# Separate use records in the linear branch, a gate with one transpose, and a new order, in a gated mix of softmax and linear attention

## The chip, the cores and the metric

The kernel runs on one core of one Trainium2 chip. The metric is device time in microseconds (us) from one execution; the median of several is compared. The core has five engines that run side by side and wait for one another by semaphores: TensorE (PE, matrix multiply), VectorE (DVE), ScalarE (ACT), GpSimd (POOL) and SyncE (SP, which issues most of the DMAs).

## The reference

One input x (2048 tokens, 512 features) goes through two attention branches with 32 heads of 16 features, and a gate mixes the results.

```python
# branch A: softmax attention
qkv = x @ wqkv                                   # 512 -> 3 * 512
p = softmax(q @ k.T * 16 ** -0.5)                # 32 heads, 2048 x 2048 each
a = (p @ v) @ wo
# branch B: linear attention; B_x is not used, x is the same
phi = lambda t: concat(softmax(t @ w_phi), softmax(-(t @ w_phi)))   # 32 features a head
kv, z = phi(k).T @ v, phi(k).sum(tokens)
b = (phi(q) @ kv / (phi(q) @ z + 1e-6)) @ wo
# gate
g = sigmoid((x * gate_w).sum(-1))
out = g * a + (1 - g) * b
```

Everything is bf16 at the inputs and the output. The bulk of it is the exponential of 32 x 2048 x 2048 scores.

## The kernel before, in words

**Softmax branch.** The scores are made transposed, keys on the partitions. A *unit* is one head's tile of 128 keys by 512 queries, one bank of PSUM. Four heads share the rows of TensorE, so four units make a *position* p; there are 512 positions (4 query chunks x 8 groups of four heads x 16 key tiles), and 2048 units. The loop runs over positions: scores (`_qk`, matmul line 988), exponential (`_exp`, line 1039), and the product with the values (`_pv`, line 1108), which adds up over the 16 key tiles of a group in one bank. Five banks are a ring for the scores; the ring is used in instructions of three and two units by turns (`GROUPS`), so ScalarE takes 1536 and 1024 columns by turns. The other three banks serve everything else.

**Units on VectorE.** A share of the units is not given to ScalarE. `SHARES` says how many of each group of 16 positions; `SOON` names four early ones. `_vector_batch` takes up to `NB` = 5 such units: line 887 scales the scores into the bits of a number (tile `vt`), `_cubic` (lines 911 to 915) makes a cubic of the fraction in `vf` and `vu`, and line 897 puts the two together. The values' product then reads `vu`. The last units of a group wait on TensorE for these tiles.

**Linear branch.** `_b_fuse` multiplies the key and query weights with `w_phi`, in place in `WB`. `_b_part` makes both softmaxes of a block of two or four token tiles on VectorE: the power of two apart from the remainder (lines 1300 and 1302, the remainder in `vf`, shared with the vector batches), a tree of maxima and one of minima (lines 1305 and 1309), their ends (line 1312, into `brec`), the differences (line 1315), a polynomial (lines 1320 to 1327), its two halves put out (lines 1329 and 1330), the sums, and their inverses. Keys come first (`_b_keys`, six calls), queries later (`_b_queries`, four calls).

**Gate.** `_gate` multiplies x with the gate's weights spread over 128 columns, a chunk of 512 tokens at a time: four matmuls into a bank, a transpose of 32 x 32 blocks on VectorE (line 805), and a copy of one column of each block (line 808). Two multiplications, an exponential on ScalarE (line 816) and an addition end it.

**The order of the work.** Nothing is written down in its final order. Each piece of work is an `Op` with an engine, a cost, a priority (`prio`, mostly the position at which it is due) and a release (`rel`, a position before which it isn't looked at). `Plan.order` then plays the execution through with these costs, engine by engine, and fixes the queue of each engine; the engines run their queues strictly in that order. `Buf` objects record who wrote and who read a tile; `Plan.op` turns the records into dependencies, also between two operations of one engine, which are waits on that engine's own semaphore. A DMA's landing is estimated in `_land`; for a plain load of `size` megabytes:

```python
self.loaded = max(o.end + 1.5, self.loaded) + o.size / 0.31
o.lat = self.loaded - o.end + (0.85 if self.loaded > 4.5 else 0.4)
```

The loads are in `_loads`. On SP, after the loads of x, come `WB` for the values (release 6) and the queries (8), the gate's weights (`gw`, release 6), the three larger pieces of the softmax weights (`WA`, columns from 128 on, release `XREL`), and the two output weights `WoA` and `WoB` (release 12). A query block of the softmax branch is projected in `_proj_q` (matmuls of line 681 into `qraw`, line 759, then eight small DMAs on SP, line 761).

The constants that the change sets: `LEAD`, `EARLY`, `SDUE` (when a vector batch is due), `QDUE`, `VPRIO`, `VREL`, `TPRIO` (when query projections, vector batches and normalisations are due), `XREL`, `KD`, `VD`, `KREL`, `VREL0` (loads and first projections), `FIRST` and `LAST` (sizes of the first and last vector batches), `OREL` (release of the last output tiles), `K0`, `SK`, `Q0`, `SQ` (positions of the linear branch's key and query parts).

Of the kernel before, what the change touches and what calls it, by code (L numbers as in the profile page):

```python
# [7 lines left out]
ALU = mybir.AluOpType  # L8
AX = mybir.AxisListType

P = 128
# [6 lines left out]
F32, BF16 = dt.float32, dt.bfloat16  # L18
# [349 lines left out]
class _Kernel:  # L368
# [46 lines left out]
    def _memory(self, ctx):  # L415
# [19 lines left out]
        self.gwb = sb("gwb", [P, 4, P], BF16)  # L435
        self.gh = sb("gh", [P, 2, NQC, 16], F32)
        self.gz = sb("gz", [P, NQC, 16], F32)
# [59 lines left out]
    def _loads(self):  # L497
# [17 lines left out]
        def load_wa(s, part, eng, prio, rel=-99):  # L515
            lo, hi = (0, P) if part == 0 else (P, D)
            self.dma(eng, f"wa{s}{part}", lambda e: e.dma_start(
                self.WA[:, s, :, lo:hi], WA3[:, :, D * s + lo:D * s + hi]), writes=[self.b_WA[s][part]], prio=prio,
                cost=0.54, rel=rel, size=0.131 if part == 0 else 0.393)

        def load_wb(s, prio, rel=-99):
# [20 lines left out]
                 writes=[self.b_gw], prio=-4, cost=0.53, rel=6, size=0.016)  # L542
# [245 lines left out]
    def _gate(self):  # L788
        op, NQC = self.plan.op, self.NQC
        b_gwb, last = Buf(), []  # L790
        op("POOL", lambda e: e.tensor_copy(self.gwb[:], self.gw[:, :, None].to_broadcast([P, 4, P])), 1.0,
           reads=[self.b_gw], writes=[b_gwb], name="gwb", prio=15)
        z = self.gz[:]
        for qc in range(NQC):
            job = Job()

            m = None
            for c in range(4):
                def mm(e, c=c, qc=qc, job=job):
                    return e.matmul(self._bank(job), self.gwb[:, c, :], self.xT[:, 4 * qc:4 * qc + 4, c],  # L800
                                    start=(c == 0), stop=(c == 3))
                m = op("PE", mm, self.c_pe(512), reads=[self.b_xT[qc], b_gwb], deps=[m], name="gate", prio=18 + qc,
                       rel=12, acquire=None if c else job)
            k = qc % 2
            t = op("DVE", lambda e, k=k, job=job: e.transpose(
                self.T1[:, k].rearrange("p b d -> p (b d)"), self._bank(job)), 0.65, deps=[m], name="gate_t",
                prio=18 + qc, writes=[self.b_T1[k]], release=job)
            last.append(op("DVE", lambda e, qc=qc, k=k: e.tensor_copy(self.gz[:, qc], self.T1[:, k, :, 0]), 0.2,
                           reads=[self.b_T1[k]], name="gate_c", prio=18 + qc))
        flat = self.gh[:].rearrange("p r q b -> p (r q b)")  # L810
        col = z.rearrange("p q b -> p (q b)")
        for r, sign in ((0, -1.0), (1, 1.0)):
            last.append(op("DVE", lambda e, r=r, sign=sign: e.tensor_scalar(
                self.gh[:, r].rearrange("p q b -> p (q b)"), col, sign, None, op0=ALU.mult), 0.2,
                deps=list(last), name="gate_z", prio=22))
# [12 lines left out]
    SHARES = (0, 2, 1, 8, 1, 8, 3, 4, 10, 3, 7, 6, 10, 4, 12, 3,  # L828
              2, 11, 10, 5, 13, 4, 7, 6, 14, 11, 4, 14, 6, 12, 14, 9)
# [5 lines left out]
    def _plan_vector(self):  # L835
# [9 lines left out]
        for k in range(n):  # L845
            at = (2 * k + 1) * 9 // (2 * n)
            self.away.append(4 * (self.NT * last + 4 * (at // 3) + at % 3 + 1) + 3)
# [328 lines left out]
    K0, SK, Q0, SQ = 17.0, 9.25, 178.0, 14.75  # L1176
    PAIRS = 8
    SOON = (8, 17, 18, 21)
    SDUE = 37

    def _branch_b(self):
# [5 lines left out]
        self.b_bsum, self.b_brec = B(), B()  # L1187
# [71 lines left out]
    def _b_part(self, s, t0, nt, slot, due):  # L1259

        op = self.plan.op
# [23 lines left out]
        rest = self.vf[:, 0:nt].rearrange("p n q -> p (n q)").rearrange("p (a v) -> p a v", v=64)  # L1285
# [12 lines left out]
        def dve(name, cost, fn, reads, writes, off=1):  # L1298
            op("DVE", fn, cost, reads=reads, writes=writes, name=name, prio=due + off)
        dve("b_grid", four(h), lambda e: e.tensor_scalar(up, signs(flat)[:, :, 0], OCTAVE, OCTAVE, op0=ALU.add,  # L1300
                                                         op1=ALU.subtract), b, [b_vt], 0)
        dve("b_rest", two(h), lambda e: e.tensor_tensor(rest, signs(flat)[:, :, 0], up, ALU.subtract), [*b, b_vt], [b_vf], 0)
        ends = ((0, ALU.max, -127.0 * 128), (1, ALU.min, 127.0 * 128))
        for s_, of, _ in ends:
            dve("b_max", two(h // 2), lambda e, s_=s_, of=of: e.tensor_tensor(tree[:, :, s_], up[:, :, 0:32], up[:, :, 32:64], of),
                [b_vt], b, 0)
        for m in (16, 8, 4):
            for s_, of, _ in ends:
                dve("b_max", two(8 * nt * m), lambda e, m=m, s_=s_, of=of: e.tensor_tensor(  # L1309
                    tree[:, :, s_, 0:m], tree[:, :, s_, 0:m], tree[:, :, s_, m:2 * m], of), b, b, 0)  # L1310
        for s_, _, bias in ends:
            dve("b_top", 0.066 + 0.0167 * nt, lambda e, s_=s_, bias=bias: e.tensor_scalar(
                top.rearrange("p (a s i) -> p a s i", s=2, i=4)[:, :, s_], tree[:, :, s_, 0:4], bias, None, op0=ALU.add),
                b, [b_brec], 0)
# [4 lines left out]
            ALU.subtract), [b_vt, b_brec], [b_vt])  # L1319
        dve("b_square", two(h), lambda e: e.tensor_tensor(even, rest, rest, ALU.mult), [b_vf], b)  # L1320
        dve("b_slope", four(h), lambda e: e.tensor_scalar(odd, even, ODD / r, 1 - ODD * c, op0=ALU.mult, op1=ALU.add),
            b, b)
        dve("b_even", four(h), lambda e: e.tensor_scalar(even, even, 128 * EVEN / r, 64 - 128 * EVEN * c,
                                                         op0=ALU.mult, op1=ALU.add), b, b)
        dve("b_odd", two(h), lambda e: e.tensor_tensor(odd, odd, rest, ALU.mult), [*b, b_vf], b)
        dve("b_part", two(h), lambda e: e.tensor_tensor(rest, even, odd, ALU.add), b, [b_vf])
        dve("b_part", two(h), lambda e: e.tensor_tensor(odd, even, odd, ALU.subtract), b, b)
        outs = signs(flat.bitcast(U16))
        dve("b_out", two(h), lambda e: e.tensor_tensor(outs[:, :, 0], down, rest, ALU.add), [b_vt, b_vf], b)
        dve("b_out", two(h), lambda e: e.tensor_tensor(outs[:, :, 1], odd, up, ALU.subtract), [b_vt, *b], b)  # L1330
# [251 lines left out]
```

## Time and profile before

| | |
|---|---|
| median of 3 runs | 840.32 us (840.21 to 841.15) |
| the profiled execution, whole | 842.38 us |
| its span, first to last instruction | 838.9 us |
| ScalarE busy | 826.7 us, 733 instructions |
| VectorE busy | 809.9 us, 1055 instructions |
| TensorE busy | 803.5 us, 8800 matmuls |
| granted TensorE clock | 1.00 |
| DMA | 20.01 MB, mean 24 GB/s |

The profile is one execution. Rows that group instructions read: line, engine, operation, output <- input, shapes, xcount | busy us, mean ns of one | idle us of the engine just before them, and what ended most of it. A record's length runs on into the next instruction's, so the distance of two starts, not the mean, is what one instruction costs in a row of them. Rows in order of time read: start, length, what, and in brackets the idle time before and what ended it. ACTq and SPq are the queues from which ACT and SP issue DMAs.

### The profile page before, as it was taken

How to read it: one execution, taken by the hardware profiler on the slowest of the kernel's cores; microseconds unless marked ns; L12 is line 12 of the kernel's file. 1: busy time of each engine (PE TensorE's matmuls, PEld its weight loads, DVE VectorE, ACT ScalarE, POOL GpSimd, SP SyncE). 2: the span in 40 equal slices, each digit the busy share in tenths (PEclk: the TensorE clock that was granted, in tenths of full speed). 3: DMA queues.
4: the chain of work that ended last, by engine and by line, in shares of the span. 5: the costliest groups of instructions: out<-in, count | busy, mean ns of one | idle time of the engine just before them, and what ended most of it. 6: DMA issues, size and time to landing. Idle time of an engine off the chain costs nothing.

```text
span 838.9 us, 19684 instructions
## 1 busy us (share of the span) xinstructions
PE 803.5 (96%) x8800; PEld 265.3 (32%) x8800; DVE 809.9 (97%) x1055; ACT 826.7 (99%) x733; POOL 8.1 (1%) x14
## 2 busy tenths in 40 slices
PE   9999999999999999999999999999999999999998
PEld 4334233233322322232223222332223332222344
DVE  5999999999999999999999989999999999999996
ACT  7999999999999999999999999999999999999997
POOL 3000000000000000000000000000000000000000
PEclk9999999999999999999999999999999999999999
DMA  9600000000000000030003000320002110000000
GB/s 227 183 1 3 5 2 7 1 2 8 2 7 2 8 1 8 2 65 19 1 15 81 14 8 2 57 52 1 8 2 52 33 32 2 2 7 2 2 2 27
DMA packets 49027, 20.01 MB, mean 24 GB/s; under 512 B 38704, under 2 KB 48944, under 8 KB 48944
## 3 DMA queue, kind: packets, MB, share of 16 engines
q1 hardware_dynamic: 48272, 18.58, 9.9%
q8 instruction: 68, 1.11, 0.6%
q10 hardware_dynamic: 672, 0.20, 0.1%
q14 instruction: 15, 0.12, 0.1%
HBM read 6.31 MB, written 2.10 MB: 10 GB/s over the span
## 4 chain that ended last, share of the span: by engine, by line
ACT 75%; DVE 16%; PE 4%; DMA 2%; SPq 2%; issue 0%
ACT ET L1039 75%; DVE vt L887 2%; DVE vu L897 2%; PE ps L988 2%; DVE vf L914 1%; DMA WA<-in_A_wqkv_dram 1%; PE ps L1117 1%; DVE vu L915 1%; DVE bq L1272 1%; DVE vf L911 1%; DMA WB<-in_B_wqkv_dram 1%; DVE vt L1315 1%; PE ps L1108 1%; SPq L604 1%; DVE bq L1309 1%; DVE V L783 1%
## 5 line engine op out<-in xcount | busy, mean ns | idle before, releaser
L1039 ACT ACTIVATE ET<-ps 128x1536 bf16<-128x1536 f32 x728 | 824.4, 1381 | 2.8 <-PE ps L988 2.3
L988 PE MATMUL ps<-qT,kT 32*128 32x512 bf16 (+2 forms) x2248 | 318.3, 364 | 26.8 <-ACT ET L1039 20.6
L1117 PE MATMUL ps<-kT,zero 128*32 128x512 bf16 (+1 forms) x3100 | 259.9, 383 | 0.0
L1108 PE MATMUL ps<-ET,V 128*32 128x512 bf16 (+2 forms) x1993 | 196.3, 364 | 0.7 <-DVE vt L887 0.4
L988 PEld LDWEIGHTS ps<-qT,kT 32*128 32x128 bf16 x2248 | 84.0, 91 | 305.0 <-ACT ET L1039 217.6
L887 DVE TENSOR_SCALAR vt<-ps 128x512 uint32<-128x512 f32 x224 | 145.1, 678 | 4.5 <-PE ps L988 4.0
L897 DVE SCALAR_TENSOR_TENSOR vu<-vt,vu 128x2560 int16<-128x2560 uint32 (+2 forms) x47 | 126.4, 2690 | 0.5
L1117 PEld LDWEIGHTS ps<-kT,zero 128*32 128x32 bf16 x3100 | 70.2, 94 | 109.0 <-issue 82.5
L1108 PE MATMUL ps<-vu,V 128*32 128x512 bf16 (+1 forms) x255 | 84.1, 360 | 0.0
L1108 PEld LDWEIGHTS ps<-ET,V 128*32 128x32 bf16 x1993 | 56.1, 95 | 58.4 <-issue 31.0
L915 DVE TENSOR_TENSOR vu<-vu,vf 128x2560 f16<-128x2560 f16 (+2 forms) x49 | 67.8, 1385 | 0.5
L914 DVE TENSOR_TENSOR vf<-vf 128x2560 f16<-128x2560 f16 (+2 forms) x49 | 67.8, 1385 | 0.2
L911 DVE TENSOR_SCALAR vf<-vt 128x2560 f16<-128x2560 uint8 (+2 forms) x47 | 66.7, 1418 | 0.0
L681 PE MATMUL ps<-WB,xT 128*128 128x512 bf16 x192 | 55.4, 383 | 1.1 <-DVE T L1161 1.0
L913 DVE TENSOR_SCALAR vu<-vf 128x2560 f16<-128x2560 f16 (+2 forms) x49 | 37.6, 767 | 0.2
L681 PE MATMUL ps<-xT,WA 128*128 128x512 bf16 (+1 forms) x124 | 35.3, 379 | 1.5 <-DMA WA<-in_A_wqkv_dram 1.3
L1108 PEld LDWEIGHTS ps<-vu,V 128*32 128x32 bf16 x255 | 22.4, 96 | 13.0 <-issue 8.4
L1161 DVE STREAM_TRANSPOSE T<-ps 128x512 f32<-128x512 f32 (+1 forms) x35 | 23.1, 660 | 2.1 <-PE ps L1108 2.0
L681 PEld LDWEIGHTS ps<-WB,xT 128*128 128x128 bf16 x192 | 14.2, 97 | 26.7 <-issue 14.4
L1272 DVE TENSOR_SCALAR bq<-ps 128x512 bf16<-128x512 f32 x32 | 21.3, 679 | 0.6 <-PE ps L681 0.5
L777 PE MATMUL ps<-WA,xT 128*128 128x128 bf16 x256 | 19.3, 220 | 0.0
L1315 DVE TENSOR_TENSOR vt<-vt,brec 128x4096 bf16<-128x4096 bf16 (+1 forms) x10 | 18.6, 1864 | 0.3
(100 smaller groups left out, 432.3 us busy)
## 6 DMA issues: line engine op xcount, KB each, us to landing
qT<-qraw SPq DMA_DIRECT2D x120, 16.0 KB, 1.8
xn<-in_A_x_dram SPq DMA_DIRECT2D x3, 512.0 KB, 6.8
WB<-in_B_wqkv_dram SPq DMA_DIRECT2D x3, 512.0 KB, 6.1
out_dram<-WB SPq DMA_DIRECT2D x12, 128.0 KB, 1.7
WA<-in_A_wqkv_dram SPq DMA_DIRECT2D x3, 384.0 KB, 8.7
xn<-in_A_x_dram SPq DMA_DIRECT2D x2, 256.0 KB, 3.8
WoA<-in_A_wo_dram SPq DMA_DIRECT2D x1, 512.0 KB, 8.3
WoB<-in_B_wo_dram SPq DMA_DIRECT2D x1, 512.0 KB, 9.0
```

The lines of the kernel that those rows point to most:

```text
L681: mm = op("PE", lambda e, c=c: e.matmul(self._bank(job)[:, 0:n], lhs(c), rhs(c), start=(c == 0), stop=(c == 3)), self.c_pe(n), reads=reads ...
L887: parts.append(op("DVE", lambda e, j=j, job=job: e.tensor_scalar(vt[:, j, :], self._bank(job), SCALE * LOG2E * 2.0 ** 24, 2.0 ** 31, op0=A ...
L897: o = op("DVE", lambda e: e.scalar_tensor_tensor(out=flat(vu).bitcast(I16), in0=flat(vt), scalar=2.0 ** -17, in1=flat(vu), op0=ALU.mult, o ...
L911: ("_frac", two, lambda e: e.tensor_scalar(vf, frac, 1 / 256, ROOT, op0=ALU.mult, op1=ALU.add), [b_vt], [b_vf]),
L913: lambda e: e.tensor_scalar(vu, vf, CUBE, SQUARE, op0=ALU.mult, op1=ALU.add), [b_vf], [b_vu]),
L914: ("_sq", two, lambda e: e.tensor_tensor(vf, vf, vf, ALU.mult), [b_vf], [b_vf]),
L915: ("_cube", two, lambda e: e.tensor_tensor(vu, vu, vf, ALU.mult), [b_vf, b_vu], [b_vu]),
L988: ins = e.matmul(out[u][:, cols], self.kT[32 * i:32 * i + 32, cp, kt * TOK:(kt + 1) * TOK], self.qT[32 * i:32 * i + 32, s, q], start=True, ...
L1039: o = plan.op("ACT", lambda e: e.activation(self.ET[:, a % NS:a % NS + n, :], self.ps[:, a % NR:a % NR + n, :], ACT.Exp, scale=SCALE), sel ...
L1108: ins = e.matmul(self._bank(ot)[32 * i:32 * i + 32, to], self.V[:, kt, g8 // 2, v0:v0 + 32], tile[:, cols], start=first and j == 0, stop=o ...
L1117: ins = e.matmul(self._bank(ot)[32 * i:32 * i + 32, lo:QCH], self.zero[:], self.kT[:, 0, lo:QCH], start=False, stop=False, tile_position=( ...
L1272: [lambda e, b, k=k: e.tensor_scalar(bq[:, k].rearrange("p (g s v) -> p g s v", g=8, s=2)[:, :, 0, :], b.rearrange("p (g v) -> p g v", g=8 ...
```

## The change

1. **Use records of the linear branch.** In `_b_part` the records of the `bq` block are split: one for the half that holds the input and the even part, one for the odd part, one for each tree, one for the ends of each tree. Operations on different halves no longer wait for one another. The instructions are the same.
2. **The query remainder** goes into `WB[:, 1]`, where the linear branch's key weights were, with a record `b_rest` that waits for the last matmul with them. Keys still use `vf`.
3. **The gate** is made in one bank: the gate's weights stand in one column of 32 of a zeroed tile, shifted by two columns for each chunk, so that sixteen matmuls add up into one bank with each chunk on a row of its own; one transpose follows, and the two multiplications read its result directly. The four column copies and the tile `gz` are gone; a memset on POOL is new.
4. **Constants and order.** All of the constants above but `K0`, `NB`, `NVU`, `VREL`, `KEEP`, `FIRST` have new values, `SHARES` is a new list (its sum is 226 instead of 224), the gate's weights are released at 12 with a later priority and counted as 0.1 MB, and the three `WA` pieces are counted as 0.45 MB instead of 0.393. `ENDS` names a 9 that stood in the code.

```diff
-    NB, NVU, LEAD = 5, 3, 11
-    QDUE, VPRIO, VREL, TPRIO = 27.0, -9.0, 161.0, 3
+    NB, NVU, LEAD = 5, 3, 13
+    QDUE, VPRIO, VREL, TPRIO = 28.0, -16.0, 161.0, 5
...
-    XREL, KD, VD = 12, 11, 5
+    XREL, KD, VD = 16, 6, 2
...
-    KREL = 2
-    EARLY = 23
-    VREL0 = 3
+    KREL = 1
+    EARLY = 31
+    VREL0 = 5
...
-    LAST = (3, 2)
-    OREL = 0
+    LAST = (4,)
+    OREL = 3
+    ENDS = 9
...
-                cost=0.54, rel=rel, size=0.131 if part == 0 else 0.393)
+                cost=0.54, rel=rel, size=0.131 if part == 0 else 0.45)
...
-                 writes=[self.b_gw], prio=-4, cost=0.53, rel=6, size=0.016)
+                 writes=[self.b_gw], prio=-0.3, cost=0.53, rel=12, size=0.1)
...
+        op("POOL", lambda e: e.memset(self.gwb[:], 0.0), 0.6, writes=[b_gwb], name="gwb_zero", prio=-10)
+        op("POOL", lambda e: e.tensor_copy(
+            self.gwb[:, :, 6:134].rearrange("p c (j r) -> p c j r", r=32)[:, :, :, 0],
+            self.gw[:, :, None].to_broadcast([P, 4, 4])), 0.3, reads=[self.b_gw, b_gwb], writes=[b_gwb], name="gwb", prio=15)
+        job, m = Job(), None
         for qc in range(NQC):
...
+                    return e.matmul(self._bank(job), self.gwb[:, c, 6 - 2 * qc:6 - 2 * qc + P],
+                                    self.xT[:, 4 * qc:4 * qc + 4, c], start=(qc + c == 0), stop=(qc + c == 6))
...
+        t = op("DVE", lambda e: e.transpose(self.T1[:, 0].rearrange("p b d -> p (b d)"), self._bank(job)), 0.65, deps=[m],
+               name="gate_t", prio=21, writes=[self.b_T1[0]], release=job)
...
-    SHARES = (0, 2, 1, 8, 1, 8, 3, 4, 10, 3, 7, 6, 10, 4, 12, 3,
-              2, 11, 10, 5, 13, 4, 7, 6, 14, 11, 4, 14, 6, 12, 14, 9)
+    SHARES = (0, 2, 2, 6, 0, 5, 4, 5, 8, 4, 9, 9, 10, 4, 15, 4,
+              2, 14, 8, 8, 12, 3, 6, 7, 14, 8, 7, 12, 6, 11, 14, 7)
...
-    K0, SK, Q0, SQ = 17.0, 9.25, 178.0, 14.75
+    K0, SK, Q0, SQ = 17.0, 8.5, 178.25, 18.0
...
-    SOON = (8, 17, 18, 21)
-    SDUE = 37
+    SOON = (16, 21, 22, 25)
+    SDUE = 33
...
+        of = self.vf[:, 0:nt]
+        if s == 0:
...
+            of, b_vf = self.WB[:, 1, 0:nt].bitcast(FP16), self.b_rest
...
+        b_x, b_odd, b_tree, b_top = Buf(), Buf(), [Buf(), Buf()], [Buf(), Buf()]
...
-                    tree[:, :, s_, 0:m], tree[:, :, s_, 0:m], tree[:, :, s_, m:2 * m], of), b, b, 0)
+                    tree[:, :, s_, 0:m], tree[:, :, s_, 0:m], tree[:, :, s_, m:2 * m], of), [b_tree[s_]], [b_tree[s_]], 0)
...
-        dve("b_square", two(h), lambda e: e.tensor_tensor(even, rest, rest, ALU.mult), [b_vf], b)
+        dve("b_square", two(h), lambda e: e.tensor_tensor(even, rest, rest, ALU.mult), [b_vf], [b_x])
...
-        dve("b_odd", two(h), lambda e: e.tensor_tensor(odd, odd, rest, ALU.mult), [*b, b_vf], b)
+        dve("b_odd", two(h), lambda e: e.tensor_tensor(odd, odd, rest, ALU.mult), [b_odd, b_vf], [b_odd])
```

More of the change, by code (lines that the diff above doesn't have):

```diff
@@ L804, in _gate, with mm @@
[L804 to L809, printed above, removed]
+                def mm(e, c=c, qc=qc):
+                    return e.matmul(self._bank(job), self.gwb[:, c, 6 - 2 * qc:6 - 2 * qc + P],
+                                    self.xT[:, 4 * qc:4 * qc + 4, c], start=(qc + c == 0), stop=(qc + c == 6))
@@ new lines, in _gate @@
+                m = op("PE", mm, self.c_pe(512), reads=[b_gwb] + (self.b_xT if m is None else []), deps=[m] if m else [], name="gate",
+                       prio=18 + qc, rel=12, acquire=None if m else job)
+        t = op("DVE", lambda e: e.transpose(self.T1[:, 0].rearrange("p b d -> p (b d)"), self._bank(job)), 0.65, deps=[m],
+               name="gate_t", prio=21, writes=[self.b_T1[0]], release=job)
+        z = self.T1[:, 0, :, 0:8].rearrange("p b (q h) -> p q b h", h=2)[:, :, :, 0]
+        last = []
@@ L1259, in _b_part @@
     def _b_part(self, s, t0, nt, slot, due):
-        op = self.plan.op
+        op, NT = self.plan.op, self.NT
         off = t0 % 4
```

59 lines of the change are left out of this document (29 added, 30 removed).

## Prediction

> **What bounds the kernel now.** I read the page first, then ScalarE in order of time over the whole span, then what TensorE did at the one large hole found there. The page's first part and its costliest group:
>
> ```profile
> PE 803.5 (96%) x8800; PEld 265.3 (32%) x8800; DVE 809.9 (97%) x1055; ACT 826.7 (99%) x733; POOL 8.1 (1%) x14
> ...
> L1039 ACT ACTIVATE ET<-ps 128x1536 bf16<-128x1536 f32 x728 | 824.4, 1381 | 2.8 <-PE ps L988 2.3
> ...
> L1117 PE MATMUL ps<-kT,zero 128*32 128x512 bf16 (+1 forms) x3100 | 259.9, 383 | 0.0
> ```
>
> ScalarE (ACT) is busy 826.7 of 838.9 us, 824.4 of that in the 728 exponentials of line 1039. TensorE's 96% holds 259.9 us of filling with zeros (line 1117), so it has room; VectorE at 97% has little. The timeline of ScalarE alone shows where its idle 12 us lie (start, length, what, and in brackets the idle time before):
>
> ```profile
> 7.33 1.45 ACT L1039 ACTIVATE ET<-ps 128x1536 bf16<-128x1536 f32 x1 [0.59 <-PE ps L988]
> 8.99 4.62 ACT L1039 ACTIVATE ET<-ps 128x1024 bf16<-128x1024 f32 x4 [0.21 <-PE ps L988]
> 13.80 15.93 ACT L1039 ACTIVATE ET<-ps 128x1024 bf16<-128x1024 f32 x14 [0.19 <-PE ps L988]
> 30.83 33.05 ACT L1039 ACTIVATE ET<-ps 128x1024 bf16<-128x1024 f32 x29 [1.10 <-PE ps L988]
> ...
> 175.25 658.73 ACT L1039 ACTIVATE ET<-ps 128x1536 bf16<-128x1536 f32 x582 [0.25 <-PE ps L988]
> 836.21 0.38 ACT L1533 ACTIVATE xT<-ps 128x256 bf16<-128x256 f32 x1 [2.22 <-PE ps L1520]
> ```
>
> The first exponential starts at 7.33, the last ends at 175.25 + 658.73 = 833.98. Between them ScalarE waits four times: 0.21 + 0.19 + 1.10 + 0.25 = 1.75 us. So the span is a head of 7.33, a chain of exponentials with 1.75 us of holes, and a tail of 838.9 - 833.98 = 4.9. Only four things can shorten it: fewer exponentials, the holes, the head, the tail. VectorE's work counts only where it makes a hole, or where it takes tiles from ScalarE.
>
> The hole of 1.10 us has a cause that the rows show. TensorE runs its queue in order:
>
> ```profile
> 27.70 0.39 PE L988 MATMUL ps<-qT,kT 32*128 32x512 bf16 x3
> ...
> 29.43 1.04 PE L681 MATMUL ps<-xT,WA 128*128 128x512 bf16 x4 [1.34 <-DMA WA<-in_A_wqkv_dram]
> ```
>
> The four matmuls at 29.43 feed the raw query tile (the next VectorE row on them is line 759), so this is the projection of query block 1. It stood 1.34 us for its weights, the scores behind it came late, and ScalarE ran dry.
>
> **The change part by part.**
>
> *Fewer tiles on ScalarE.* The share list of before adds up to 224, that of after to 226; with the four early tiles, 228 become 230 of 2048 on VectorE. ScalarE keeps 1820, then 1818. They go in groups of three and two by turns: 1820 is 364 pairs of groups, 728 instructions; 1818 is 363 pairs and a group of three, 727. One instruction of two tiles goes. Its length from three successive starts:
>
> ```profile
> 400.73 2.63 ACT L1039 ACTIVATE ET<-ps 128x1024 bf16<-128x1024 f32 x2
> 401.63 2.64 ACT L1039 ACTIVATE ET<-ps 128x1536 bf16<-128x1536 f32 x2
> 402.96 2.65 ACT L1039 ACTIVATE ET<-ps 128x1024 bf16<-128x1024 f32 x2
> ```
>
> From 400.73 to 401.63 is 0.90 us for two tiles (the three-tile one takes 1.33). **Term: -0.90.**
>
> *The load order.* The issues on the SP queue in order of time, and below them the page's times from issue to landing (the last number of a row):
>
> ```profile
> 19.04 0.53 SPq L540 DMA_DIRECT2D gw<-in_gate_w_dram  x1
> 19.61 0.51 SPq L522 DMA_DIRECT2D WB<-in_B_wqkv_dram  x1
> 20.16 3.54 SPq L517 DMA_DIRECT2D WA<-in_A_wqkv_dram  x3
> 23.75 0.61 SPq L544 DMA_DIRECT2D WoA<-in_A_wo_dram  x1
> 24.40 1.27 SPq L578 DMA_DIRECT2D WoB<-in_B_wo_dram  x1
> ```
>
> ```profile
> WoA<-in_A_wo_dram SPq DMA_DIRECT2D x1, 512.0 KB, 8.3
> WoB<-in_B_wo_dram SPq DMA_DIRECT2D x1, 512.0 KB, 9.0
> ...
> gw<-in_gate_w_dram SPq DMA_DIRECT2D x1, 1.0 KB, 5.2
> ```
>
> With XREL 16 the three WA loads are released after WoA, WoB and the gate weights (all released at 12), so these may stand ahead of them. WoA landed at 23.75 + 8.3 = 32.05, WoB at 24.40 + 9.0 = 33.4: 1.35 us for each such load. Two more of them ahead put WA 2.7 us later on the chip. The plan's own estimate moves more: behind WB it counted 0.016 + 0.524 + 0.393 + 0.393 up to the second WA load, and now 0.524 + 0.524 + 0.524 + 0.1 + 0.45 + 0.45; at the 0.31 a us of its code that is 4.3, then 8.3 us, 4.0 later. So the projection is placed 4.0 us later and its weights land 2.7 later: the wait of 1.34 comes to about 0.04. Block 1 is first used at position 32 of 512, near 7.33 + 32 x 1.61 = 59 us, so the delay itself starves nothing. The bounds: the hole goes wholly (-1.10), or it grows by the 2.7 (a rival below). It is nearest to the first, by that sum. **Term: -1.10.** What is late next on ScalarE are the waits of 0.19 to 0.25; KD and VD move the projections behind two of them, bounds -0.40 and +0.5 (as large again), taken as 0.
>
> *VectorE's load.* The rows of one tile's work, then the gate's and the trees':
>
> ```profile
> L887 DVE TENSOR_SCALAR vt<-ps 128x512 uint32<-128x512 f32 x224 | 145.1, 678 | 4.5 <-PE ps L988 4.0
> L897 DVE SCALAR_TENSOR_TENSOR vu<-vt,vu 128x2560 int16<-128x2560 uint32 (+2 forms) x47 | 126.4, 2690 | 0.5
> L915 DVE TENSOR_TENSOR vu<-vu,vf 128x2560 f16<-128x2560 f16 (+2 forms) x49 | 67.8, 1385 | 0.5
> L914 DVE TENSOR_TENSOR vf<-vf 128x2560 f16<-128x2560 f16 (+2 forms) x49 | 67.8, 1385 | 0.2
> L911 DVE TENSOR_SCALAR vf<-vt 128x2560 f16<-128x2560 uint8 (+2 forms) x47 | 66.7, 1418 | 0.0
> L913 DVE TENSOR_SCALAR vu<-vf 128x2560 f16<-128x2560 f16 (+2 forms) x49 | 37.6, 767 | 0.2
> ...
> L1309 DVE TENSOR_TENSOR bq<-bq 128x256 bf16<-128x256 bf16 (+3 forms) x60 | 16.7, 278 | 1.2
> ...
> L1312 DVE TENSOR_SCALAR brec<-bq 128x128 bf16<-128x128 bf16 (+1 forms) x20 | 3.7, 187 | 0.5
> ...
> L805 DVE STREAM_TRANSPOSE T<-ps 128x512 f32<-128x512 f32 x4 | 2.9, 712 | 0.1
> ...
> L808 DVE COPY gz<-T 128x16 f32<-128x16 f32 x4 | 0.7, 164 | 0.0
> ```
>
> A tile costs (145.1 + 126.4 + 66.7)/224 + (67.8 + 67.8 + 37.6)/228 = 2.27 us; two more are +4.5. The gate drops three of four transposes (2.2) and the four copies (0.7): -2.9. The records save waits between instructions of VectorE itself, whose price is in two pairs, one that waits for its forerunner and one that doesn't:
>
> ```profile
> 510.98 1.22 DVE L1320 TENSOR_TENSOR bq<-vf 128x2048 f16<-128x2048 f16 x1
> 512.24 0.69 DVE L1321 TENSOR_SCALAR bq<-bq 128x2048 f16<-128x2048 f16 x1
> ...
> 190.48 1.22 DVE L1320 TENSOR_TENSOR bq<-vf 128x2048 f16<-128x2048 f16 x1
> 191.62 0.68 DVE L759 CAST qraw<-ps 128x512 bf16<-128x512 f32 x1
> ```
>
> The next start comes 1.26 us after line 1320 when it needs its result, 1.14 when it doesn't: 0.12 a wait, of which 0.04 shows as idle. The trees and maxima (lines 1309, 1312) show 1.2 + 0.5 = 1.7 us idle, some 42 waits, so about 5 us in all; the bounds are 0 (other work fills every wait, as at 190.48) and ten calls x some 12 instructions x 0.12 = 14. I take 5, from the idle row. Balance: 4.5 - 2.9 - 5 = -3.4 us, with ends +1.6 and -12.8. None of it touches ScalarE while VectorE keeps its due times, so it enters the sum as 0.
>
> The Trainium skill, in "VectorE: DVE Perf Modes", section "The DRAIN you can't avoid", says that chained VectorE instructions cost the same with or without a semaphore between them. The pairs above don't bear this out: 0.12 us apart. By that rule the records would save nothing and the balance would be +1.6 us; the sum for ScalarE would be the same as long as the slack in the third rival below holds that.
>
> *The rest, at nothing.* The query remainder in the key weights' place adds no instruction; its wait is for the key matmuls of the linear branch, whose last part is due at position 17 + 8.5 x 12 = 119, the first query part at 178; without that cover VectorE would wait, and rival 3 has the price. The gate's sixteen matmuls stay, in one bank held longer instead of four in turn; the pool memset and copy lie on an engine busy 8.1 us. The gate's weights land later, but they landed at 19.04 + 5.2 = 24.2 and the first transpose of the gate ran at 41.7:
>
> ```profile
> L805 DVE STREAM_TRANSPOSE T<-ps x4: 707/713/717, 41.7 to 57.6; 128x512 f32<-128x512 f32 x4
> ```
>
> That is 17 us of cover; without it normalisation waits first, not ScalarE. The last batches and the later output tiles touch the tail only through TensorE; the 4.9 us there follow the last exponential (accumulate, transpose, normalise, project, store) and keep their length.
>
> *Sum* against the profiled execution: 842.38 - 0.90 - 1.10 = 840.38. It stands 2.06 above the median of the runs, 840.32, and I carry that over: **838.3 us**, -0.24%.
>
> **The rivals.**
> 1. *The hole stays.* If the plan still puts the projection as much too early as now, only the term of -0.90 is left: 839.4, -0.11%. For it: the plan missed this landing by 1.34 us with five loads ahead, and now more stand ahead.
> 2. *The weights come later still (slower).* If the projection keeps its place in TensorE's queue while WoA and WoB go first, its wait is 1.34 + 2.7 = 4.0 us and ScalarE's hole 1.10 + 2.7 = 3.8: 840.32 - 0.90 + 2.7 = 842.1, +0.21%. It turns slower where that hole passes 1.10 + 0.90 + 1.68 = 3.7. Against it: the plan counts those two loads as well.
> 3. *VectorE comes late.* Shares of groups 9 to 19 grow from 70 to 83 tiles, 13 x 2.27 = 29.5 us, against query parts moved back. VectorE's spare time is thin except here (stretch, its length, TensorE, weight loads, VectorE, ScalarE, ...):
>
> ```profile
> 480.00:500.00 20.00, 18.67 (x190) 5.14 (x188) 18.11 (x19) 20.00 (x19) 0.00 (x0) 1.00 0.03 8
> 500.00:520.00 20.00, 18.55 (x214) 5.47 (x215) 18.61 (x25) 20.00 (x19) 0.00 (x0) 1.00 0.01 2
> ```
>
> That is 1.89 + 1.39 = 3.3 us. One batch late by its last instruction (2.7 us) stops the accumulation on TensorE and the scores behind it: 838.3 + 2.7 = 841.0. Against it: the balance of -3.4, and even +1.6 fits in 3.3.
> 4. *The small holes go too*: -0.21 - 0.19 - 0.25, 837.7.
>
> **How the numbers follow.** Forecast 0.45, rival 1 0.25, rival 2 0.12, rival 3 0.10, rival 4 0.08. A measurement of this kernel can tell about 0.2% (1.68 us) from no change, so the bounds are 838.64 and 842.00. The forecast lies only 0.3 inside, so 0.05 of it goes to "same"; rival 3 is split evenly. Faster 0.40 + 0.08 = 0.48; same 0.25 + 0.05 + 0.05 = 0.35; slower 0.12 + 0.05 = 0.17. The range runs from rival 4 less the 0.59 ahead of the first exponential (837.1) to just below rival 2 (842.0), which leaves out that rival and little else.
>
> **What would show it.** Right: 727 exponentials with some 823.5 us; no wait of TensorE for WA near 30 us, and holes on ScalarE between first and last exponential of 0.5 to 1 us; transposes of line 805's successor x1; fewer idle tenths before the tree's instructions. Wrong: a wait for WA or another load over 1 us on TensorE (rivals 1 and 2), waits of line 1108 or 988 for VectorE's tiles in groups 9 to 19 (rival 3), or a tail over 4.9 us.

## Result, and the profile after

| | before | after |
|---|---|---|
| median of the runs | 840.91 us (840.21 to 843.18, 6 runs) | 837.99 us (837.14 to 838.51, 6 runs) |
| ratio, 95% interval | | 0.9963 (0.9952 to 0.9974) |
| profiled execution, span | 842.38, 838.9 us | 838.33, 836.5 us |

The change makes the kernel 0.37% faster. The forecast was 838.3 us. The time came out as forecast; of the two terms behind it one was too large and one too small, and a third that I had entered as zero is not zero. Lines have moved: exponential 1039 is 1035, scores 988 are 984, zero filling 1117 is 1113, trees 1309 and 1312 are 1315 and 1318, the gate's transpose 805 is 803.

The page of after, its first part and the same two groups as before:

```profile
PE 792.9 (95%) x8711; PEld 263.0 (31%) x8753; DVE 806.8 (96%) x1050; ACT 825.4 (99%) x733; POOL 8.0 (1%) x15
...
L1035 ACT ACTIVATE ET<-ps 128x1536 bf16<-128x1536 f32 x728 | 823.1, 1397 | 1.7 <-PE ps L984 1.5
...
L1113 PE MATMUL ps<-kT,zero 128*32 128x512 bf16 (+1 forms) x3052 | 255.3, 383 | 0.0
```

There are still 728 exponentials, not 727. ScalarE's groups of after, with different shapes kept apart, say why, and VectorE's groups say where the tile went:

```profile
L1035 ACT ACTIVATE ET<-ps 128x1536 bf16<-128x1536 f32 x364 | 585.8, 1609 | 0.9 <-PE ps L984 0.8
L1035 ACT ACTIVATE ET<-ps 128x1024 bf16<-128x1024 f32 x363 | 430.4, 1186 | 0.8 <-PE ps L984 0.7
...
L1035 ACT ACTIVATE ET<-ps 128x512 bf16<-128x512 f32 x1 | 0.8, 752 | 0.0
```

```profile
L883 DVE TENSOR_SCALAR vt<-ps 128x512 uint32<-128x512 f32 x226 | 148.3, 681 | 3.8 <-PE ps L984 3.1
...
L1315 DVE TENSOR_TENSOR bq<-bq 128x256 bf16<-128x256 bf16 (+3 forms) x60 | 13.2, 278 | 0.0
...
L1318 DVE TENSOR_SCALAR brec<-bq 128x128 bf16<-128x128 bf16 (+1 forms) x20 | 3.1, 189 | 0.0
...
L803 DVE STREAM_TRANSPOSE T<-ps 128x512 f32<-128x512 f32 x1 | 0.7, 709 | 0.0
```

364 x 3 + 363 x 2 + 1 = 1819 tiles on ScalarE. VectorE makes 226 and the four early ones: 1819 + 230 = 2049, one more than the 2048 units. A share of 15 in group 14 meets only 14 places, and one unit is named twice; VectorE makes it twice. So one tile left ScalarE, not two: a two-tile instruction became a one-tile one. The rest of VectorE is as forecast: one gate transpose, and no idle time before the trees and their ends, where before showed 1.2 and 0.5 us.

ScalarE in order of time (start, length, what, count, idle time before):

```profile
7.35 44.61 ACT L1035 ACTIVATE ET<-ps 128x1536 bf16<-128x1536 f32 x39 [0.50 <-PE ps L984]
...
51.94 194.75 ACT L1035 ACTIVATE ET<-ps 128x1024 bf16<-128x1024 f32 x172
247.39 109.50 ACT L1035 ACTIVATE ET<-ps 128x1024 bf16<-128x1024 f32 x97 [0.70 <-PE ps L984]
357.20 474.44 ACT L1035 ACTIVATE ET<-ps 128x1536 bf16<-128x1536 f32 x420 [0.31 <-PE ps L984]
833.86 0.38 ACT L1544 ACTIVATE xT<-ps 128x256 bf16<-128x256 f32 x1 [2.22 <-PE ps L1531]
```

The holes of the first 50 us, 0.21, 0.19 and 1.10 in before, are gone. Two others have come, 0.70 and 0.31, so holes count 1.01 us against 1.75. Head (7.35) and tail (836.5 - 357.20 - 474.44 = 4.9) are as before. The 0.70 has a cause in TensorE's rows of after:

```profile
245.66 0.60 PE L984 MATMUL ps<-qT,kT 32*128 32x512 bf16 x2 [0.80 <-DMA qT<-qraw]
```

The scores of a query block stood 0.80 us for the block's small DMAs. No rival had named that.

The large hole went as forecast, but not by the small margin that I had worked out. SP's queue of after, and TensorE at the same projection:

```profile
17.09 1.22 SPq L522 DMA_DIRECT2D WB<-in_B_wqkv_dram  x2
18.35 0.51 SPq L544 DMA_DIRECT2D WoA<-in_A_wo_dram  x1
18.90 0.51 SPq L578 DMA_DIRECT2D WoB<-in_B_wo_dram  x1
19.45 0.87 SPq L540 DMA_DIRECT2D gw<-in_gate_w_dram  x1
28.46 1.61 SPq L1227 DMA_TRANSPOSE WT<-WB  x1
30.11 1.73 SPq L517 DMA_DIRECT2D WA<-in_A_wqkv_dram  x3
```

```profile
37.12 0.39 PE L984 MATMUL ps<-qT,kT 32*128 32x512 bf16 x2
37.44 1.04 PE L681 MATMUL ps<-xT,WA 128*128 128x512 bf16 x4
```

The `WA` pieces stand not only behind the output weights but behind the transpose of the linear query weights, and go out 10 us later (30.11 against 20.16). The projection of block 1 stands 8.0 us later (37.44 against 29.43), without a wait. The loads also land faster, by the page of after (the last number is the time from issue to landing):

```profile
WA<-in_A_wqkv_dram SPq DMA_DIRECT2D x3, 384.0 KB, 5.2
...
WoA<-in_A_wo_dram SPq DMA_DIRECT2D x1, 512.0 KB, 5.7
WoB<-in_B_wo_dram SPq DMA_DIRECT2D x1, 512.0 KB, 6.6
```

The same row of before for `WA`:

```profile
WA<-in_A_wqkv_dram SPq DMA_DIRECT2D x3, 384.0 KB, 8.7
```

`WA` took 8.7, `WoA` 8.3 and `WoB` 9.0 in before. There the gate's weights stood ahead of all five; but in after the two output weights also have no `WA` piece ahead of them any more, and `WA` goes out when they have landed. These rows don't tell the one cause from the other.

**Waits that no row shows as idle.** The holes fell by 0.74 us, and the span by 2.4. The rest lies inside ScalarE's rows. A record of three tiles is 1.61 us long, and the next instruction starts 1.33 after it; the records overlap, and a wait shorter than the overlap of about 0.27 us leaves no bracket. It can be seen from the long rows. In before, 582 exponentials run from 175.25 for 658.73 us without a bracket. They are 291 pairs, and a pair takes 2.235 us from start to start in the rows at 400.73 to 402.96 (0.904 + 1.331): 650.4 us. Some 8 us are somewhere in between. I therefore took the starts of all 728 exponentials and subtracted 1.333 us for each instruction of three tiles and 0.907 for each of two, the usual distances; what is left is called **excess** below, in us. With the 1.331 and 0.904 of the rows above every sum would be some 1.8 us larger; the differences stay.

| kernel | starts before 50 us | the rest | sum |
|---|---|---|---|
| before | 2.43 | 8.76 | 11.19 |
| after | 0.49 | 8.59 | 9.08 |

So the span's 2.4 us are 1.94 in the first 50 us, 0.17 in the rest, and 0.27 from the last exponential (0.75 us in place of 1.02); head and tail together change nothing. The medians differ by a little more, 2.9: what lies outside the span is 1.8 us in the runs of after, and 2.15 in the median of before's runs on the chips of the experiments (3.48 in its first profiled execution). I found no cause for that part.

### The profile page after: what moved, and what is told of

It reads as the page before. It is cut to its first block, busy times and chain, and to the rows that moved or that the text cites. A ratio compares the mean times of both kernels' runs of the same rounds, so it can differ in the third digit from the quotient of the medians.

```text
span 836.5 us, 19540 instructions
## 1 busy us (share of the span) xinstructions
PE 792.9 (95%) x8711; PEld 263.0 (31%) x8753; DVE 806.8 (96%) x1050; ACT 825.4 (99%) x733; POOL 8.0 (1%) x15
## 4 chain that ended last, share of the span: by engine, by line
ACT 92%; DVE 5%; PE 2%; DMA 0%; SPq 0%; issue 0%
ACT ET L1035 92%; DVE vt L883 1%; PE ps L984 0%; DMA qT<-qraw 0%; SPq L761 0%; PE ps L633 0%; DVE vu L893 0%; PE ps L1113 0%; DVE bq L1268 0%; DVE vt L1321 0%; DVE VB L1252 0%; DVE T L1157 0%; DVE vf L907 0%; DVE vu L911 0%; DVE vf L910 0%; DVE bq L1315 0%
## 5 line engine op out<-in xcount | busy, mean ns | idle before, releaser
L1113 PE MATMUL ps<-kT,zero 128*32 128x512 bf16 (+1 forms) x3052 | 255.3, 383 | 0.0
L883 DVE TENSOR_SCALAR vt<-ps 128x512 uint32<-128x512 f32 x226 | 148.3, 681 | 3.8 <-PE ps L984 3.1
L893 DVE SCALAR_TENSOR_TENSOR vu<-vt,vu 128x2560 int16<-128x2560 uint32 (+3 forms) x47 | 127.6, 2716 | 0.7
L1113 PEld LDWEIGHTS ps<-kT,zero 128*32 128x32 bf16 x3052 | 67.9, 94 | 103.2 <-issue 78.5
L910 DVE TENSOR_TENSOR vf<-vf 128x2560 f16<-128x2560 f16 (+3 forms) x49 | 68.6, 1400 | 0.6
L911 DVE TENSOR_TENSOR vu<-vu,vf 128x2560 f16<-128x2560 f16 (+3 forms) x49 | 68.5, 1398 | 0.5
L907 DVE TENSOR_SCALAR vf<-vt 128x2560 f16<-128x2560 uint8 (+3 forms) x47 | 67.1, 1427 | 0.2
L681 PE MATMUL ps<-WB,xT 128*128 128x512 bf16 x165 | 48.8, 383 | 4.0 <-issue 1.6
L909 DVE TENSOR_SCALAR vu<-vf 128x2560 f16<-128x2560 f16 (+3 forms) x49 | 37.9, 774 | 2.0 <-PE ps L1104 1.8
```

What stands on the lines that cost most here:

```text
L681: mm = op("PE", lambda e, c=c: e.matmul(self._bank(job)[:, 0:n], lhs(c), rhs(c), start=(c == 0), stop=(c == 3)), self.c_pe(n), reads=reads ...
L883: parts.append(op("DVE", lambda e, j=j, job=job: e.tensor_scalar(vt[:, j, :], self._bank(job), SCALE * LOG2E * 2.0 ** 24, 2.0 ** 31, op0=A ...
L893: o = op("DVE", lambda e: e.scalar_tensor_tensor(out=flat(vu).bitcast(I16), in0=flat(vt), scalar=2.0 ** -17, in1=flat(vu), op0=ALU.mult, o ...
L907: ("_frac", two, lambda e: e.tensor_scalar(vf, frac, 1 / 256, ROOT, op0=ALU.mult, op1=ALU.add), [b_vt], [b_vf]),
L909: lambda e: e.tensor_scalar(vu, vf, CUBE, SQUARE, op0=ALU.mult, op1=ALU.add), [b_vf], [b_vu]),
L910: ("_sq", two, lambda e: e.tensor_tensor(vf, vf, vf, ALU.mult), [b_vf], [b_vf]),
```

## The experiments

The theory at this point: the gain is the load order's, at the start; use records, gate and tiles are worth little by themselves. Rivals: the records give it; the new order gives it; nothing in particular, since any re-planned order moves by as much.

**Only the gate's weights load later.** In before's code one line changes; the queues of all engines but SP are then the same as in before.

```diff
-                 writes=[self.b_gw], prio=-4, cost=0.53, rel=6, size=0.016)
+                 writes=[self.b_gw], prio=-0.3, cost=0.53, rel=12, size=0.016)
```

> The kernel before with one edit: the load of the gate's weights (512 pieces of two bytes) goes behind the two output weights on the SP queue; every other queue is unchanged. If the small pieces hold up the loads behind them, the weights for query block 1 land about 2 us earlier than 29.4, TensorE's wait of 1.34 us and ScalarE's hole of 1.10 us go, and the time falls by 1.1 us (-0.13%). If the plan is only wrong about the rate, the wait stays within 0.3 us and the time is the same. If the gain came from VectorE, the time is the same too.

Measured: 840.0 us (839.49 to 841.72) beside 840.63; ratio 0.9995 (0.9986 to 1.0003). SP's queue, TensorE, and the landing from the page of this kernel:

```profile
19.72 1.87 SPq L517 DMA_DIRECT2D WA<-in_A_wqkv_dram  x3
...
24.33 1.13 SPq L540 DMA_DIRECT2D gw<-in_gate_w_dram  x1
```

```profile
28.10 1.04 PE L681 MATMUL ps<-xT,WA 128*128 128x512 bf16 x4
...
41.60 0.38 PE L1240 MATMUL ps<-wphi,WT 128*128 128x128 bf16 x4 [0.59 <-DVE T L805]
```

```profile
WA<-in_A_wqkv_dram SPq DMA_DIRECT2D x3, 384.0 KB, 6.4
```

The `WA` pieces are issued 0.44 us earlier, issuing the three takes 1.87 us instead of 3.54, and TensorE's wait of 1.34 us is gone. The 6.4 and the 8.7 of before are medians of three pieces. All three, in the order of their issue, in before and here:

```profile
DMA to landing us min/median/max: 6.7/8.7/8.9
```

```profile
DMA to landing us min/median/max: 5.8/6.4/8.6
```

The projection waits for the second: it lands at 26.7 us instead of 29.4, the other two only 1.4 and 1.2 us earlier. What the gate's weights do to the DMA engines shows between 21 and 24 us, in before and here (the last two numbers are the engines' share and GB/s):

```profile
21.00:24.00 3.00, 3.00 (x29) 1.15 (x26) 2.43 (x4) 3.00 (x4) 0.00 (x0) 1.00 0.77 237
```

```profile
21.00:24.00 3.00, 3.00 (x30) 1.15 (x30) 2.36 (x4) 3.00 (x4) 0.00 (x0) 1.00 1.08 368
```

In these 3 us before's trace has the 512 packets of two bytes of the gate's weights (by line 540, one for each value), and 237 GB/s are moved instead of 368. By these rows the load of 1 KB costs what stands behind it about 1.1 us (an estimate: 131 GB/s are missing for 3 us, and before moves 350 GB/s from 24 to 27 us), and `WoB`, the last, lands 1.1 us earlier here. The Trainium skill, in "DMA: Bandwidth & Descriptors", section "Specifications", gives 512 bytes as the smallest transfer for the full rate; the trace agrees, with 237 in place of 368 GB/s. The second `WA` piece gains more, 2.7 us. In before 2.5 us lie between the landings of the first and the second piece and 1.2 between the second and the third, here 1.2 and 2.7; why one distance is longer, and which one, is open. The prediction and the plan's estimate went by the size of the loads ahead, where this one counts next to nothing (0.016 MB). But the gate's weights aren't the whole cause either: two kernels below leave them ahead and don't wait. Not all of the hole's 1.10 us is gained: the gate now comes later, TensorE waits 0.59 us for its transpose, and ScalarE has a new hole:

```profile
42.35 20.62 ACT L1039 ACTIVATE ET<-ps 128x1536 bf16<-128x1536 f32 x18 [0.34 <-PE ps L988]
```

The medians differ by 0.6 us, and the interval takes in no change at all.

**Only the records, in an unchanged order.** The plan is made with the old records; then the queue of every engine and every bank is kept as it is, and the waits alone come from the new records. The remainder stays in `vf`.

```diff
+            q = p.order() if guide is None else p.follow(guide)
...
+        if self.fine:
+            return self._b_part_fine(s, t0, nt, slot, due)
...
+        dve("b_odd", two(h), lambda e: e.tensor_tensor(odd, odd, rest, ALU.mult), [b_odd, b_vf], [b_odd])
```

> The kernel before with its order held fast on every engine; only the waits inside the linear branch are those of the new use records (the remainder stays where it was). If the gain came from the loads, the time is the same within 0.4 us; VectorE's idle time ahead of the trees and maxima falls from 1.7 us to under 0.3, and its waits of 0.12 us each go, some 5 us in all. If the gain came from VectorE's waits, 1 to 2 us go (-0.12 to -0.24%).

Measured: 839.88 us (839.27 to 840.87) beside 840.63; ratio 0.9990 (0.9981 to 0.9999). The page's first part, VectorE's trees and TensorE's wait for `WA` in this kernel:

```profile
PE 796.8 (95%) x8760; PEld 265.2 (32%) x8800; DVE 806.4 (96%) x1055; ACT 826.2 (99%) x733; POOL 8.3 (1%) x14
```

```profile
L1431 DVE TENSOR_TENSOR bq<-bq 128x256 bf16<-128x256 bf16 (+3 forms) x60 | 13.8, 273 | 0.0
```

```profile
29.39 1.04 PE L716 MATMUL ps<-xT,WA 128*128 128x512 bf16 x4 [0.84 <-DMA WA<-in_A_wqkv_dram]
```

VectorE is busy 3.5 us less with the same 1055 instructions, and the 1.7 us of idle time before the trees are gone: 5.2 us, where the prediction had 5. By the traces VectorE waits on its own semaphore 464 times here and 509 times in before, so 45 waits went, 0.12 us each. The Trainium skill's rule on chained instructions ("VectorE: DVE Perf Modes", "The DRAIN you can't avoid") would have left both numbers unchanged; this trace differs from it, as the two pairs did. But the prediction entered this at 0, and it isn't: the time falls by some 0.75 us, between the two expectations. The wait for `WA` has no part in that: it is 0.84 instead of 1.34 us because the first exponential of this execution began 0.56 us later, and the projection starts at the same time (29.39 and 29.43). The gain lies away from the start, where the excess fell from 8.76 to 7.87. That VectorE's earlier tiles shorten waits of TensorE, and so of ScalarE, that were too short to be seen is the likely way; no row shows it.

**Both together, in an unchanged order.** The same with the gate's load late.

> The kernel before with its order held fast, with the new records' waits and with the gate's weights loaded last. If the two direct gains (0.6 and 0.8 us by the medians of the first runs) add up, the time falls by 1.1 to 1.7 us (-0.13 to -0.20%), and the three first holes on ScalarE, but the one of 1.10 us, are as before. If they share one cause, it falls by 0.8 us at most.

Measured: 839.26 us (838.83 to 840.35) beside 840.92; ratio 0.9979 (0.9971 to 0.9988). ScalarE in order of time:

```profile
7.42 6.19 ACT L1074 ACTIVATE ET<-ps 128x1536 bf16<-128x1536 f32 x5 [0.49 <-PE ps L1023]
13.80 28.14 ACT L1074 ACTIVATE ET<-ps 128x1024 bf16<-128x1024 f32 x25 [0.19 <-PE ps L1023]
42.10 20.48 ACT L1074 ACTIVATE ET<-ps 128x1536 bf16<-128x1536 f32 x18 [0.16 <-PE ps L1023]
...
62.63 769.35 ACT L1074 ACTIVATE ET<-ps 128x1536 bf16<-128x1536 f32 x680
```

The two gains add up, and the hole that the late gate made has shrunk from 0.34 to 0.16. The excess of the four kernels that share before's order, and of after:

| kernel | before 50 us | the rest | sum |
|---|---|---|---|
| before | 2.43 | 8.76 | 11.19 |
| gate's load late | 1.36 | 8.73 | 10.09 |
| records | 1.83 | 7.87 | 9.70 |
| both | 1.19 | 7.90 | 9.09 |
| after | 0.49 | 8.59 | 9.08 |

"Both" reaches after's excess to 0.01 us: from the first exponential's start to the last one's both kernels take 823.54 us, before 825.64. So two small edits in the old order bring ScalarE as much as the whole new order does. They don't show that the new order gains by the same waits: after has 0.70 less than "both" before 50 us and 0.69 more in the rest, so the equal sums are partly luck. The first column also moves with the start of the one execution that was profiled (first exponentials at 7.33, 7.50, 7.89, 7.42 and 7.35 us, in the table's order). After has besides it one tile less (0.27 us) and the smaller part outside the span (1.8 against 2.15 us in the median).

**The new order with the old waits.** In after's code, each VectorE instruction of the linear branch waits for the one before it of that branch; the order is after's.

```diff
-            for o in p.order()["PE"]:
+            queues = p.order()
+            last = None
+            for o in queues["DVE"]:
+                if o.name.startswith("b_"):
+                    if last is not None and last not in o.deps:
+                        o.deps.append(last)
+                    last = o
+            for o in queues["PE"]:
```

> The changed kernel with its order held fast; each VectorE instruction of the linear branch waits again for the one of that branch in front of it. By the loads, this stays within 0.5 us of the changed kernel (838.0 to 838.5). By VectorE's waits, the gain of the records is given back: 1.5 us or more above the changed kernel (839.5 and up).

Measured: 851.13 us (850.96 to 851.48) beside 840.63; ratio 1.0122 (1.0108 to 1.0136). The page's first part, and the group of waits of ScalarE that grew:

```profile
PE 793.3 (93%) x8711; PEld 262.5 (31%) x8753; DVE 816.6 (96%) x1050; ACT 828.5 (98%) x733; POOL 8.0 (1%) x15
```

```profile
ACT ET L1042 <- PE ps L991: 10.6, 20, 1.0
```

Twenty visible holes, none over 1.0 us, and an excess of 21.72 us, spread over the span. But this chain is stronger than the old records. VectorE is busy 9.8 us more than in after (816.6 against 806.8), where the records in the old order had taken away 3.5; by the queues that the kernels build, it waits for the instruction just in front of it 228 times here and 107 times in after, 170 times in before and 106 times in before's order with the records. So the run shows that the new order has no room for that much more VectorE time in the linear branch. What exactly the old records would cost in it is not shown.

**One part at a time, planned anew.** Three kernels take one part of the change and let the plan make its own order: the records and the remainder's place in before; the gate in before; and after with the old load order.

```diff
-    XREL, KD, VD = 16, 6, 2
+    XREL, KD, VD = 12, 6, 2
...
-                cost=0.54, rel=rel, size=0.131 if part == 0 else 0.45)
+                cost=0.54, rel=rel, size=0.131 if part == 0 else 0.393)
...
-                 writes=[self.b_gw], prio=-0.3, cost=0.53, rel=12, size=0.1)
+                 writes=[self.b_gw], prio=-4, cost=0.53, rel=6, size=0.016)
```

Records and remainder:

> The kernel before with the new records and the remainder's new place, all constants and shares as before, and the order planned anew from them. If the records are worth something by themselves, the time falls by 0.8 us or more. If the gain hangs on an order fitted to them, the old constants don't fit and the time rises, by 2 us or more, with small waits of ScalarE all over the span.

Measured: 850.7 us (850.24 to 852.5) beside 840.92; ratio 1.0122 (1.0108 to 1.0136). I had expected the price of a worse fit to be small waits all over. It is one place. ScalarE, and TensorE just before:

```profile
190.47 1.45 ACT L1039 ACTIVATE ET<-ps 128x1536 bf16<-128x1536 f32 x1 [7.02 <-PE ps L1108]
```

```profile
186.90 1.07 PE L777 MATMUL ps<-WA,xT 128*128 128x128 bf16 x16 [3.00 <-DVE T L1161]
```

A value projection stands in TensorE's queue for a bank that a normalisation's transpose on VectorE has yet to free, and the product with the values (line 1108), for which ScalarE waits, stands behind it. Of the 10 us, 7.0 are this hole; three more for the same line, 0.99, 1.91 and 1.48, follow up to 210 us.

The gate:

> The kernel before with the new gate alone, the order planned anew. By VectorE's work 2.9 us go from its queue before 65 us: if that reaches ScalarE, the time falls by 0.5 us or more. If it lies beside other work, the change is only what the new order brings, within 2 us either way, and it shows after the gate, not at it.

Measured: 841.31 us (840.47 to 842.46) beside 840.92; ratio 1.0006 (0.9996 to 1.0015). The start gains (excess before 50 us 0.91 in place of 2.43), and the tail gives it back:

```profile
836.49 0.39 ACT L1528 ACTIVATE xT<-ps 128x256 bf16<-128x256 f32 x1 [3.79 <-PE ps L1515]
```

This start bears on the load order too. The gate's weights stand ahead of `WA` as in before, and yet TensorE doesn't wait at the projection:

```profile
18.64 0.56 SPq L539 DMA_DIRECT2D gw<-in_gate_w_dram  x1
...
19.80 2.99 SPq L516 DMA_DIRECT2D WA<-in_A_wqkv_dram  x3
```

```profile
28.34 1.04 PE L680 MATMUL ps<-xT,WA 128*128 128x512 bf16 x4
```

The `WA` pieces go out 0.36 us earlier than in before, and the second lands 6.5 us after its issue, at 26.9 us, where before's landed at 29.4. The DMA engines pay for the small packets as in before (253 GB/s between 21 and 24 us). In the kernels that issue `WA` at 20.16 to 20.55 us with the gate's weights ahead (before, the records in before's order, records and remainder, and the one due time below), TensorE waits 0.84 to 1.34 us. So moving the gate's weights ends the wait in before's order, but it isn't the only way, and what else decides isn't shown.

After with the old load order:

> The changed kernel with the loads' release, priority and sizes as before, the order planned anew. If the loads' wait alone is given back, the time is 1.0 to 1.9 us above the changed kernel (839 to 840). If the order hangs on every constant, it is several us above it, with waits far from the loads.

Measured: 853.96 us (850.63 to 856.13) beside 840.92; ratio 1.0143 (1.0119 to 1.0168). Of its waits the largest is again for TensorE's product with the values, 11.6 us in three holes:

```profile
ACT ET L1035 <- PE ps L1104: 11.6, 3, 6.2
```

This kernel doesn't measure the load order. It measures an order made anew from constants that were set for another; and its four runs spread from 850.63 us at a granted clock of 1.000 to 856.13 at 0.992, which is the profiled one. At its start, with the gate's weights ahead, `WA` lands in 6.9 us (median) and TensorE doesn't wait for it.

**How much an order alone moves.** Before, with one due time changed:

```diff
-    QDUE, VPRIO, VREL, TPRIO = 27.0, -9.0, 161.0, 3
+    QDUE, VPRIO, VREL, TPRIO = 27.0, -9.0, 161.0, 4
```

> The kernel before with one constant changed, TPRIO 4 instead of 3: no work is added or removed, only the priority of the normalisations' transposes moves by one position, and the order is planned anew. If orders differ little, the time is the same within 0.8 us. If each order has its own waits, it moves by 1 to 3 us, and the constants of before were the better ones: slower.

Measured: 842.3 us (842.15 to 844.46) beside 840.82; ratio 1.0017 (1.0008 to 1.0027). One new hole, and a tail longer by 0.55:

```profile
571.58 263.63 ACT L1039 ACTIVATE ET<-ps 128x1024 bf16<-128x1024 f32 x233 [0.93 <-PE ps L988]
```

The instructions are those of before and the waits follow from the order; the time moved by 1.5 us.

**The tiles.** After with shares of 14 and 5 in place of 15 and 4 (really 1818 tiles for ScalarE, 727 exponentials), and after with 14 in place of 15 (no unit made twice, still 1819 tiles).

```diff
-    SHARES = (0, 2, 2, 6, 0, 5, 4, 5, 8, 4, 9, 9, 10, 4, 15, 4,
+    SHARES = (0, 2, 2, 6, 0, 5, 4, 5, 8, 4, 9, 9, 10, 4, 14, 5,
```

> The changed kernel with a share of 14 instead of 15 in group 14 and 5 instead of 4 in group 15. In the changed kernel one tile of group 14 is made twice on VectorE, so ScalarE keeps 1819 tiles; here it keeps 1818 and 727 instructions. By the tile count alone the time falls by 0.2 to 0.5 us against the changed kernel (837.5 to 837.8). If each new order brings its own waits, it lies anywhere within 1.5 us of it.

Measured: 838.65 us (838.31 to 839.52) beside 840.63; ratio 0.9975 (0.9964 to 0.9986). The hole at 247.39 us has gone, and two others have come:

```profile
591.34 1.02 ACT L1035 ACTIVATE ET<-ps 128x1024 bf16<-128x1024 f32 x1 [0.71 <-PE ps L984]
592.94 238.75 ACT L1035 ACTIVATE ET<-ps 128x1536 bf16<-128x1536 f32 x211 [0.58 <-PE ps L984]
```

> The changed kernel with a share of 14 instead of 15 in group 14, so that no tile is made twice: VectorE has 2.3 us less to do, ScalarE keeps the same 1819 tiles; the order is planned anew. If VectorE's time reaches ScalarE, it is 0.3 to 1 us below the changed kernel (837.0 to 837.7, ratio near 0.995). If only the order counts, it lies within 1.5 us of it on either side.

Measured: 838.68 us (837.48 to 840.51) beside 840.82; ratio 0.9971 (0.9961 to 0.9981). Its four runs at a granted clock of 1.000 took 837.48 to 838.81 us, the four at 0.996 to 0.998 took 838.67 to 840.51; after's six were all at 1.000. Neither kernel beats after by its interval. The unit that VectorE makes twice costs it one tile (busy 806.8 us with it, 804.2 without), and nothing that can be seen at the end.

## Why the prediction was right, point by point

- **The bound** held. ScalarE's exponentials are the chain before and after, and every change of the span was found ahead of the first, between their starts, at the last one, or in the tail. What lies outside the span is not in it, 0.35 us between before and after. VectorE's work counted only through waits.
- **Fewer tiles, -0.90**, was mis-sized. One tile left ScalarE, not two, and it shortened the last instruction: -0.27. The share list has to be held against the places that a group has, not only added up.
- **The load order, -1.10**, was right in its direction and too small: the first 50 us lost 1.94 us of excess, the hole of 1.10 and the small waits around it. My reason was partly another. I had the plan's shift (4.0 us) just covering the chip's (2.7). In fact the projection went 8.0 us later and the piece that it needs landed 6.6 us later, at 36.0, so 1.5 us were to spare. The one-line experiment shows a price that I had not seen: the gate's weights cost the loads behind them about 1.1 us. A row that I had quoted held the hint: the three issues of `WA` took 3.54 us, the one of `WB` 0.51. But two kernels with the gate's weights ahead don't wait either, so how much of after's start is due to their place is not shown.
- **VectorE's balance, -3.4**, came out near: busy time fell by 3.1 us, and 1.7 us of idle time before the trees went too, 4.8 together. That it "touches ScalarE" not at all failed: in the unchanged order the records give a ratio of 0.9990 (0.9981 to 0.9999).
- **Rival 1** (hole stays) and **rival 2** (weights later still) didn't come: there is no wait for `WA`. What rival 2 rested on, a projection that keeps its place while its weights move, is refuted by the row at 37.44.
- **Rival 3** (VectorE late) didn't come. With 9.8 us more for VectorE in the linear branch the same order is 1.22% slower than before (ratio 1.0108 to 1.0136), by twenty visible waits and not by one late batch; so VectorE can make this order late, but whether the old records would have is not shown. The shares that grow from 70 to 83 are those of groups 10 to 19, not 9 to 19, and one of the 13 is the unit made twice.
- **Rival 4** (small holes go too) came in part: 0.21, 0.19 and 0.25 went, 0.70 and 0.31 came elsewhere.

The errors, +0.63 in the tiles and -0.84 at the start, nearly cancel. The forecast's time was better than its terms. There is luck in the level too: the forecast change of -2.0 us is a ratio of 0.9976, just outside the measured interval (0.9952 to 0.9974), and the time agrees because the median of before is 840.91 us in six runs and not the 840.32 from which the prediction started.

What stays open: "both" is at 0.9979 and after at 0.9963. One tile and the part outside the span are worth 0.27 + 0.35 = 0.6 us of that 1.3; the intervals overlap, and the rest was not separated. Of the 1.94 us at the start, the late gate's weights alone brought 1.07 in before's order and with the records 1.24; what the new order adds there was not taken apart. Nor is it known why a kernel's part outside the span is 1.8 us in the median in after and the seven other kernels whose order isn't before's, and 2.15 in the four that share before's. The remainder's place was not tried without the records.

## What to carry to other kernels

Where a planner fixes the order, test one part of a change with the order held fast: planned anew, the records (with the remainder's place) lost 1.2%, and in the old order they gained 0.1%. Measure a busy engine by the distance of its starts, not by its idle time, and sum what exceeds the usual distance by stretches of the span. Look at the loads made of many tiny pieces, however few bytes they have, when something waits for a load behind them: here 512 pieces of two bytes cost about 1.1 us of transfer.

## What the runs showed that I had not expected

- ScalarE shows 99% busy, and its starts still exceed their usual distances by some 9 to 11 us, of which the rows show 1.0 to 1.8 as idle; a wait shorter than the overlap of its records (1.61 us long, 1.33 apart) isn't seen.
- That excess belongs to the order: before and the kernel with the gate's load late agree to 0.03 us in each stretch of 50 us from 50 us on (0.76 and 0.76 from 250 to 300, 0.17 and 0.17 from 300 to 350), although they are different executions.
- One load of 1 KB brought the DMA engines down to 237 GB/s for 3 us, where 368 were moved without it, and with it the issue of the three loads behind took 3.54 us instead of 1.87. The landing that mattered came 2.7 us later; in the kernel with the new gate alone, with the same load ahead, it did not.
- 45 waits between instructions of one engine cost VectorE 5.2 us, 0.12 each.
